# The blocks of w1 by halves of F, and another order of splits, ranks and the tile table around the first tiles

## The chip, the cores and the metric

One NeuronCore of a Trainium2 chip runs the whole kernel, which is written by hand for its five engines: TensorE (PE, matmuls; PEld is its load of weights), VectorE (DVE), ScalarE (ACT), GpSimd (POOL) and SyncE (SP, which here issues DMAs). The metric is the device time in microseconds, the median of several runs.

## The reference

Pooled attention, a routed layer with one expert for each token, and a routed layer with two, in float32:

```python
x = attention(q, pooled k, pooled v)       # 8 x 576 tokens, 512 wide
e = argmax(x @ w_gate + bias); g = softmax(...)[e]
x = g * (relu(x @ w1[e]) @ w2[e])          # layer 1, 8 experts, F = 1024
n = x @ w_gate2 + log1p(exp(x @ w_noise)) * noise
for e in top 2 of n: out += p[e] * (relu(x @ w1b[e]) @ w2b[e])   # layer 2
```

## The kernel before

**Tiles.** Attention runs over 36 tiles of 128 tokens (`t`). Each ends in `av(t)`, whose VectorE part makes `xr` (in two halves) and the gate's logits `lg`, and in `store_x(t)`, a DMA of 256 KB into `x_d`, issued from ScalarE's queue one step later. The gate works by five groups of tiles: `gate_a` makes the one-hot matrix `goh` (VectorE), `gate_b1` the exp (ScalarE) and the ranks (small matmuls, L864 and L866), `gate_b2` and `gate_c` scatter each token's entry into the list `l1_d`. From the list and a table of tiles, the tokens of one expert are gathered 128 at a time: `us[k]`, called tile k here, 37 tiles in layer 1 and 76 in layer 2.

**One tile.** `gather_tile` (GpSimd: copy `cur` out of the list, gather `x`, and in layer 1 gather `nz` and take five small steps), `xT` (transposes of x on TensorE), `g1(u, hf)` for the two halves of F, `hT` or `hT_pe` (transposes of h), `g2` (in the program of the next tile), `finish` (ScalarE: `yo` and the first part of x3; GpSimd: `xr`; SP: a store of yo). The gate of layer 2 needs the result in three bf16 parts: `rest_b` (ScalarE), `rest_c` (GpSimd, L358), `x2T` (SP: the DMA transpose `x3t`), `logits2` (TensorE, L371). Every product of float32 matrices is made of three matmuls of parts (`mm3`, L294 to L296), so every block of weights is split into a high part (ScalarE) and a low part (VectorE for the first expert, GpSimd later): `split_pair` for the first expert's blocks, two at a time, `split_w` for one block of a later one.

**The first expert's weights** are loaded by pairs of blocks (`load_pair`, 512 KB on SP) into three staging buffers `sg`; w1 has pairs 0 to 3, and so has w2. A fourth pair waits for a buffer. w1's high and low parts stand where the buffers of attention's loads were, w2's where attention's other buffers were, the four `xr` among them.

**What sets the order.** The program's order is that of every engine's queue; waits between engines are semaphores, and a waiting instruction holds up all behind it on its engine. The attention loop (from L987) calls the splits of w1 at t = 33, 34 and 35:

```python
for i in {34: (1, 2), 35: (3,)}.get(t, ()):
    split_w1(i)
...
if t == 33:
    split_w1(0)
```

Tiles 0 to 3 are in `opening(k)`: g1 of tile k, with other steps at fixed places, then g2 and finish of tile k-1, hT_pe of tile k, and the three parts of tile k-1. `pre(k)` gathers tile k by the table (a generator; its first step is the gather of x), `prew(k)` loads a weight block. The table of tiles is a generator of small VectorE steps, `tab1`, up to "pe", where TensorE transposes it (L613) and VectorE copies it into `row`; registers of POOL, ACT and SP are loaded from `row` (L174). In `opening(2)` the rest of tab1, pre(4), prew(3) and prew(4) come ahead of g2 of tile 1.

Of the kernel before, what the change touches and what calls it, by code (L numbers as in the profile page):

```python
# [41 lines left out]
def kernel(ctx: ExitStack, tc: tile.TileContext, a: dict):  # L42
# [182 lines left out]
    def load_pair(u, src, j, k):  # L225
        u.sg = stg.tile([P, 2, 512], F32, name="sg")
        nc.sync.dma_start(u.sg, wpair[ds(src + j, 2), :, k, :].rearrange("j p f -> p j f"))
# [70 lines left out]
    def g1(u, hf):  # L298
        if hf == 0:
            u.h = mk.tile([P, F], F32, name="h", bufs=1)  # L300
        p = bank(hf)
        for c in range(4):
            s = slice(c * P, (c + 1) * P)
            mm3(p, u.xh[:, s], u.xl[:, s], 0, u.par + (2 * c + hf), c == 0, c == 3, u.reads)
        A.activation(u.h[:, 512 * hf:512 * hf + 512], p, AF.Relu)  # L305
# [149 lines left out]

    def load_list(src):
        nc.sync.dma_start(lst.rearrange("p c k -> p (c k)"), src.rearrange("(p c) k -> p (c k)", p=P))
# [8 lines left out]
    def first_expert():  # L466
        c = const.tile([P, E], F32, name="fc")
        V.tensor_tensor(c, base1, ebase8, op=OP.subtract)
        m = const.tile([P, 8], F32, name="fm")
        V.max(m, c)  # L470
        ix = const.tile([P, 8], mybir.dt.uint32, name="fix")
        V.max_index(ix, m, c)
        e0 = const.tile([P, 1], F32, name="fe")
        V.tensor_copy(e0, ix[:, 0:1])
        ei = const.tile([1, 2], I32, name="fei")
        V.tensor_scalar(ei[:, 0:1], e0[0:1, :], float(CPE), None, op0=OP.mult)
        V.tensor_scalar(ei[:, 1:2], e0[0:1, :], 8.0, None, op0=OP.mult)
        V.tensor_scalar(p8, iota8, e0, None, op0=OP.subtract)
        V.tensor_scalar(c, p8, 0.0, 8.0, op0=OP.is_lt, op1=OP.mult)
        V.tensor_tensor(p8, p8, c, op=OP.add)  # L480
        V.tensor_scalar(first8, p8, 0.0, None, op0=OP.is_equal)
        return reg(ei[0:1, 0:1], [ET.SP], 7 * CPE), reg(ei[0:1, 0:1], [ET.Pool], 7 * CPE), reg(ei[0:1, 1:2], [ET.SP], 56)

    def tables(layer, base, res, tag=""):
# [128 lines left out]
        nc.tensor.transpose(tp[0:12, 0:P], tab, ident)  # L613
        sc = w.tile([1, 4 + K2], I32, name="sc" + L)
# [17 lines left out]
        yield  # L632
        row = w.tile([6, P], I32, name="row" + L)
        V.tensor_copy(row, tp[0:6, 0:P])
# [49 lines left out]
    with actx:  # L684
# [172 lines left out]

        def gate_b1(g):
            n = GS[g]
            lg, oh = gs[g]  # L860
            A.activation(lg, lg, AF.Exp)
# [74 lines left out]
        def pick_first():  # L936
            at["col"], at["col_p"], at["w"] = first_expert()
# [9 lines left out]
        def load_w1(i):  # L947
# [3 lines left out]
            load_pair(pairs[0][i], at["w"], 2 * i, 0)  # L951
# [39 lines left out]
        for t in range(NT):  # L991
# [4 lines left out]
            for i in {34: (1, 2), 35: (3,)}.get(t, ()):  # L996
                split_w1(i)
# [6 lines left out]
            if t == 33:  # L1004
# [83 lines left out]
    def opening(k):  # L1088
# [9 lines left out]
        if k != 2:  # L1098
            xT(us[k + 1])
        if k == 0:  # L1100
            gate_b1(NG - 1)
        if k == 3:
            split_w(u, 0, u.dst, u.eng)
# [3 lines left out]
        if k == 3:  # L1107
            drain(gate)
        if k == 0:
            gate_b2(NG - 1)  # L1110
# [3 lines left out]
            for i in range(3):  # L1114
                split_pair(pairs[1][i], 2 * i, 1, V)
            load_list(l1_d)
# [4 lines left out]
        if k == 1:  # L1121
            split_pair(pairs[1][3], 6, 1, V)
            drain(until(tab1, "pe"))
        if k == 2:
            drain(tab1)
            drain(pre(4))
            prew(3)
            prew(4)
# [9 lines left out]
        finish(v)  # L1138
        if k == 3:
# [7 lines left out]
        if k == 1:  # L1147
            us[K1].dense = K1
            late = gather_tile(us[K1], lst, at["col_p"] + K1, 1)
# [8 lines left out]
        drain(late)  # L1158

# [140 lines left out]
def host_arrays(inp):  # L1300
# [41 lines left out]
    for g, (w1, w2) in enumerate((("moe_w1", "moe_w2"), ("moe2_w1", "moe2_w2"))):  # L1342
# [3 lines left out]
        w[8 * g:8 * g + 8, :, :, 0] = u.reshape(8, 4, P, 2, 512).transpose(0, 1, 3, 2, 4).reshape(8, 8, P, 512)  # L1346
# [18 lines left out]
```

## Time and profile before

| | |
|---|---|
| median of 3 timed runs | 1483.0 us (1481.58 to 1483.82) |
| the profiled execution | 1486.63 us, its span 1484.9 us |
| mean granted TensorE clock | 0.996 |
| PE, PEld busy | 98%, 81% |
| DVE, ACT, POOL busy | 80%, 81%, 61% |

Times in the profile's rows are microseconds from the span's start. In a timeline the columns are start, duration, engine, line, operation, output <- input, shapes and number of instructions, and in brackets the idle time of the engine ahead of it with what ended it. "issue" is a wait that the profile shows no cause of. A matmul of 128x512 starts some 0.23 us behind the one before; its own duration is longer, since they overlap.

### The profile page before, as it was taken

Reading aid. Unit: us, or ns where it says so; the run is one execution under the profiler, and the core shown is the slowest. Engines: PE = TensorE matmul, PEld = TensorE weight load, DVE = VectorE, ACT = ScalarE, POOL = GpSimd, SP = SyncE. Lnnn points to the kernel's source line nnn. Section 1 sums busy time; section 2 is a strip of 40 time slices with the busy share of each in tenths; the row PEclk is TensorE's granted clock in tenths of the full one; section 3 lists DMA queues with packets and bytes.
Section 4 is the critical chain, followed back from the end, with each engine's and each line's share of the span. In section 5 each row is a group of like instructions: output and inputs, shape, how many; then the busy total and the mean of one; then the engine's idle time right before and its main releaser. Section 6 shows DMA issues by size and latency. Waiting matters only on the chain.

```text
span 1484.9 us, 31025 instructions
## 1 busy us (share of the span) xinstructions
PE 1449.0 (98%) x7485; PEld 1209.0 (81%) x7485; DVE 1181.0 (80%) x2995; ACT 1200.2 (81%) x3153; POOL 900.5 (61%) x1064
## 2 busy tenths in 40 slices
PE   7998899999999999999999999999999999999997
PEld 6988788888888888778888888888888888888886
DVE  6776767777777777779888888888888888888884
ACT  5766559888888888878888888888888888888883
POOL 7677568888888887665544544445445445444452
PEclk9999999999999999999999999999999999999999
DMA  8965555655555554444344344443443443434432
GB/s 320 339 222 181 187 137 146 161 161 147 142 140 140 142 142 135 132 101 107 89 107 93 88 106 93 100 98 89 107 93 86 107 93 92 102 92 104 94 88 45
DMA packets 136891, 191.10 MB, mean 129 GB/s; under 512 B 71376, under 2 KB 95184, under 8 KB 134032
## 3 DMA queue, kind: packets, MB, share of 16 engines
q1 hardware_dynamic: 102240, 129.67, 29.2%
q0 software_dynamic: 24688, 49.94, 17.2%
q10 hardware_dynamic: 9792, 9.44, 1.9%
q8 instruction: 80, 1.31, 0.4%
q14 instruction: 91, 0.75, 0.2%
HBM read 121.64 MB, written 52.82 MB: 117 GB/s over the span
## 4 chain that ended last, share of the span: by engine, by line
issue 36%; PE 33%; POOL 15%; DVE 4%; POOLq 4%; ACT 4%; DMA 2%; SPq 0%; another core or an unknown queue 0%; ACTq 0%; DVEq 0%
PE bank L294 8%; PE bank L296 8%; PE bank L295 8%; POOL out L453 8%; POOL w2l L223 5%; PE bank L817 3%; POOLq L174 3%; PE bank L332 2%; ACT xt L289 2%; PE bank L771 2%; PE bank L798 1%; DMA x_d<-xr 1%; POOLq L223 1%; DVE g2t L393 1%; POOL cur L244 1%
## 5 line engine op out<-in xcount | busy, mean ns | idle before, releaser
L312 DVE STREAM_TRANSPOSE ht<-h 32x256 f32<-32x256 f32 x1136 | 495.4, 436 | 95.9 <-ACT h L305 81.3
L289 ACT ACTIVATE xt<-xz 32x128 f32<-32x128 f32 x1728 | 531.4, 308 | 34.6 <-DVE xz L282 13.5
L294 PE MATMUL bank<-w1h,xh 128*128 (+1 forms) x904 | 357.3, 395 | 0.0
L295 PE MATMUL bank<-w1l,xh 128*128 (+1 forms) x904 | 354.6, 392 | 0.0
L296 PE MATMUL bank<-w1h,xl 128*128 (+1 forms) x904 | 353.7, 391 | 0.0
L296 PE MATMUL bank<-w2h,hl 128*128 (+1 forms) x896 | 351.7, 393 | 0.1
L295 PE MATMUL bank<-w2l,hh 128*128 (+1 forms) x896 | 351.4, 392 | 0.0
L294 PE MATMUL bank<-w2h,hh 128*128 (+1 forms) x896 | 350.6, 391 | 0.0
L223 POOL TENSOR_TENSOR w1l<-sg,w1h 128x512 f32 x109 | 140.7, 1291 | 237.5 <-ACT w1h L220 231.3
L453 POOL DMA_INDIRECT out<-yo,cur x76 | 121.1, 1593 | 163.4 <-ACT yo L450 155.9
L296 PEld LDWEIGHTS bank<-w2h,hl 128*128 128x128 f32 x896 | 168.3, 188 | 39.7 <-DVE hl L321 3.3
L296 PEld LDWEIGHTS bank<-w1h,xl 128*128 128x128 f32 x904 | 169.8, 188 | 36.8
L294 PEld LDWEIGHTS bank<-w1h,xh 128*128 128x128 f32 x904 | 169.7, 188 | 36.3
L295 PEld LDWEIGHTS bank<-w1l,xh 128*128 128x128 f32 x904 | 169.9, 188 | 35.2
L294 PEld LDWEIGHTS bank<-w2h,hh 128*128 128x128 f32 x896 | 168.3, 188 | 37.2
L295 PEld LDWEIGHTS bank<-w2l,hh 128*128 128x128 f32 x896 | 168.3, 188 | 36.4
L305 ACT ACTIVATE h<-bank 128x512 f32<-128x512 f32 x226 | 133.0, 589 | 68.5 <-PE bank L296 59.8
L223 POOL TENSOR_TENSOR w2l<-sg,w2h 128x512 f32 x109 | 141.5, 1298 | 14.3 <-ACT w2h L220 14.3
L250 POOL DMA_INDIRECT x<-x_d,cur x113 | 124.1, 1098 | 37.7 <-POOL cur L244 33.4
L320 ACT ACTIVATE hh<-ht 128x1024 fp32r<-128x1024 f32 x71 | 75.4, 1062 | 58.6 <-DVE ht L312 30.6
L278 DVE TENSOR_TENSOR xl<-xt,xh 128x512 fp32r<-128x512 f32 x108 | 77.2, 715 | 56.0 <-ACT xh L274 43.4
L187 POOL DMA_INDIRECT l_d<-le,dst x74 | 80.1, 1083 | 28.8 <-issue 12.3
(269 smaller groups left out, 1979.2 us busy)
## 6 DMA issues: line engine op xcount, KB each, us to landing
sg<-w SPq DMA_DIRECT2D x118, 512.0 KB
out<-zt SPq DMA_DIRECT2D x37, 256.0 KB
x_d<-yo SPq DMA_DIRECT2D x37, 256.0 KB
x_d<-xr ACTq DMA_DIRECT2D x36, 256.0 KB
kk<-kT SPq DMA_DIRECT2D x7, 1152.0 KB
q<-qT SPq DMA_DIRECT2D x7, 1152.0 KB
vv<-vT SPq DMA_DIRECT2D x7, 1152.0 KB
x_d<-zt SPq DMA_DIRECT2D x10, 256.0 KB
```

What stands on the lines that cost most here:

```text
L187: ins = G.indirect_dma_start(out=dram_t, out_offset=bass.IndirectOffsetOnAxis(ap=ix, axis=0), in_=src, in_offset=None, bounds_check=P * LC ...
L223: eng.tensor_tensor(l, u.sg[:, k, :], h.bitcast(F32), op=OP.subtract)
L250: G.indirect_dma_start(out=u.x, out_offset=None, in_=src[0:top, :], in_offset=off, bounds_check=top - 1, oob_is_err=True)
L278: V.tensor_tensor(u.xl, p, u.xh.bitcast(F32), op=OP.subtract)
L289: A.activation(u.xt[32 * q:32 * q + 32, :, 32 * i:32 * i + 32], zv[:, q], AF.Copy)
L294: nc.tensor.matmul(p, hs, rh, start=first, stop=False)
L295: nc.tensor.matmul(p, hs, rl, start=False, stop=False)
L296: nc.tensor.matmul(p, ls, rh, start=False, stop=last)
L305: A.activation(u.h[:, 512 * hf:512 * hf + 512], p, AF.Relu)
L312: V.transpose(out=t[32 * q:32 * q + 32, :, 32 * i:32 * i + 32], in_=hv[:, q])
L320: A.activation(u.hh, u.t, AF.Copy)
L453: G.indirect_dma_start(out=out_d, out_offset=bass.IndirectOffsetOnAxis(ap=u.ci[:, 2:3], axis=0), in_=u.yo, in_offset=None, bounds_check=N ...
```

## The change

It reorders the host's array of w1 so that blocks 0 to 3 hold half 0 of F and blocks 4 to 7 half 1 (`u.par + 4 * hf + c`); pair 3 of w1 is loaded into the buffer named ht instead of a staging buffer. Pair 0 is split behind av(34), pairs 1 to 3 ahead of av(35). In `opening(0)` the exp of the last gate group and the first two splits of w2 stand ahead of g1's second half, the ranks behind it, and the last two splits behind hT_pe. A new DMA, `load_column`, brings the list's column for tile 3's gather. In `opening(1)` the table's last steps are at the end; in `opening(2)` the rest of the table, pre(4), prew(3) and prew(4) are behind finish of tile 1; in `opening(3)` xT of tile 4 and the first split of tile 3's block are behind g1's second half. `row` is copied ahead of the table's last scalars. Left out below are that copy's place and a register of POOL that is no longer loaded:

```diff
@@ -222,8 +222,11 @@
             h = block(W[2 * k], dst, 0.5)
         eng.tensor_tensor(l, u.sg[:, k, :], h.bitcast(F32), op=OP.subtract)
 
-    def load_pair(u, src, j, k):
-        u.sg = stg.tile([P, 2, 512], F32, name="sg")
+    def load_pair(u, src, j, k, own=False):
+        if own:
+            u.sg = mk.tile([P, 8, P], F32, name="ht", bufs=1).rearrange("p (j k) f -> p j (k f)", j=2)
+        else:
+            u.sg = stg.tile([P, 2, 512], F32, name="sg")
         nc.sync.dma_start(u.sg, wpair[ds(src + j, 2), :, k, :].rearrange("j p f -> p j f"))
 
     def split_pair(u, j, k, eng):
...
@@ -301,7 +304,7 @@
         p = bank(hf)
         for c in range(4):
             s = slice(c * P, (c + 1) * P)
-            mm3(p, u.xh[:, s], u.xl[:, s], 0, u.par + (2 * c + hf), c == 0, c == 3, u.reads)
+            mm3(p, u.xh[:, s], u.xl[:, s], 0, u.par + (4 * hf + c), c == 0, c == 3, u.reads)
         A.activation(u.h[:, 512 * hf:512 * hf + 512], p, AF.Relu)
 
     def hT(u):
...
@@ -452,6 +455,11 @@
     def add_out(u):
         G.indirect_dma_start(out=out_d, out_offset=bass.IndirectOffsetOnAxis(ap=u.ci[:, 2:3], axis=0),
                              in_=u.yo, in_offset=None, bounds_check=N + P - 1, oob_is_err=True, compute_op=OP.add)
+
+    def load_column():
+        col4 = const.tile([P, 8], F32, name="fm")[:, 0:4].rearrange("p (c k) -> p c k", c=1)
+        nc.sync.dma_start(col4, l1_d.rearrange("(p c) k -> p c k", p=P)[:, ds(at["col"] + K1, 1), :])
+        return col4
 
     def load_list(src):
         nc.sync.dma_start(lst.rearrange("p c k -> p (c k)"), src.rearrange("(p c) k -> p (c k)", p=P))
...
@@ -855,10 +862,15 @@
             gate_b1(g)
             gate_b2(g)
 
+        def gate_e(g):
+            lg, oh = gs[g]
+            A.activation(lg, lg, AF.Exp)
+
         def gate_b1(g):
             n = GS[g]
             lg, oh = gs[g]
-            A.activation(lg, lg, AF.Exp)
+            if g < NG - 1:
+                gate_e(g)
             pr = bank(7)[:, 0:(n + 1) * E].rearrange("p (t e) -> p t e", e=E)
             for t in range(n):
                 nc.tensor.matmul(pr[:, t + 1:, :], ones, oh[:, t:t + 1, :].to_broadcast([P, n - t, E]),
...
@@ -948,7 +960,7 @@
             if i == 0:
                 rctx.close()
                 open_w(0, "right")
-            load_pair(pairs[0][i], at["w"], 2 * i, 0)
+            load_pair(pairs[0][i], at["w"], 2 * i, 0, i == 3)
 
         def split_w1(i):
             split_pair(pairs[0][i], 2 * i, 0, V)
...
@@ -993,15 +1005,15 @@
                 transp(t)
             if t == NT - 1:
                 xT(early[0])
-            for i in {34: (1, 2), 35: (3,)}.get(t, ()):
-                split_w1(i)
+                for i in (1, 2, 3):
+                    split_w1(i)
             scores(t + 3, 0)
             maxes(t + 3, 0)
             expo(t + 2)
             if t:
                 store_x(t - 1)
                 av(t)
-            if t == 33:
+            if t == NT - 2:
                 split_w1(0)
             scores(t + 3, 1)
             maxes(t + 3, 1)
...
@@ -1095,37 +1107,37 @@
                 next(gate)
             drain(pr)
         g1(u, 0)
-        if k != 2:
+        if k < 2:
             xT(us[k + 1])
         if k == 0:
-            gate_b1(NG - 1)
+            gate_e(NG - 1)
+            for i in (0, 1):
+                split_pair(pairs[1][i], 2 * i, 1, V)
         if k == 3:
-            split_w(u, 0, u.dst, u.eng)
             drain(until(gate, "tail"))
             xblocks(us[5])
         g1(u, 1)
         if k == 3:
+            xT(us[4])
+            split_w(u, 0, u.dst, u.eng)
             drain(gate)
         if k == 0:
+            gate_b1(NG - 1)
             gate_b2(NG - 1)
             for n in range(GS[-1]):
                 gate_c(NG - 1, n)
             hT_pe(u)
-            for i in range(3):
+            at["col4"] = load_column()
+            load_list(l1_d)
+            for i in (2, 3):
                 split_pair(pairs[1][i], 2 * i, 1, V)
-            load_list(l1_d)
             for n in range(12):
                 next(tab1)
             return
         late = iter(())
         if k == 1:
-            split_pair(pairs[1][3], 6, 1, V)
-            drain(until(tab1, "pe"))
-        if k == 2:
-            drain(tab1)
-            drain(pre(4))
-            prew(3)
-            prew(4)
+            for n in range(6):
+                next(tab1)
         if k == 3:
             drain(xshift(us[5]))
             xhigh(us[5], flat(us[5].xt))
...
@@ -1136,6 +1148,11 @@
             xT(us[3])
         g2(v, range(4, 8))
         finish(v)
+        if k == 2:
+            drain(tab1)
+            drain(pre(4))
+            prew(3)
+            prew(4)
         if k == 3:
             xblocks(us[6])
             hT_pe(u)
...
@@ -1146,7 +1163,7 @@
         hT_pe(u)
         if k == 1:
             us[K1].dense = K1
-            late = gather_tile(us[K1], lst, at["col_p"] + K1, 1)
+            late = gather_tile(us[K1], at["col4"], 0, 1)
         elif k == 2:
             late = pre(5)
         next(late, None)
...
@@ -1156,6 +1173,8 @@
             logits2(us[0])
         x2T(v)
         drain(late)
+        if k == 1:
+            drain(until(tab1, "pe"))
 
     def gated(k):
         u, v = us[k], us[k - 1] if k else None
...
@@ -1343,7 +1362,7 @@
         u = inp[w1]
         if g == 0:
             u = u.reshape(8, 2, 4, D, F).transpose(0, 1, 3, 2, 4)
-        w[8 * g:8 * g + 8, :, :, 0] = u.reshape(8, 4, P, 2, 512).transpose(0, 1, 3, 2, 4).reshape(8, 8, P, 512)
+        w[8 * g:8 * g + 8, :, :, 0] = u.reshape(8, 4, P, 2, 512).transpose(0, 3, 1, 2, 4).reshape(8, 8, P, 512)
         w[8 * g:8 * g + 8, :, :, 1] = inp[w2].reshape(8, 8, P, 512)
     r["w"] = w
     return {k: np.ascontiguousarray(v) for k, v in r.items()}
```

ScalarE's queue around half 1 of tile 0. `w1h` and `w2h` are the high parts in splits of pairs, `x_d<-xr` the stores of x, `lg<-lg` the exp of the gate, `h<-bank` relu of one half, `hh<-bank` the high part of h's transposes. Before:

```order
L231 ACTIVATE w1h<-sg 128x1024
L828 DMA x_d<-xr 256x1x256 x2
L305 ACTIVATE h<-bank_2534 128x512
L274 ACTIVATE xh<-bank_2548 128x512
L861 ACTIVATE lg<-lg 128x40
L305 ACTIVATE h<-bank_2565 128x512
L334 ACTIVATE hh<-bank_2616 128x512
L334 ACTIVATE hh<-bank_2623 128x512
L231 ACTIVATE w2h<-sg 128x1024 x3
```

and now:

```order
L234 ACTIVATE w1h<-ht 128x1024
L835 DMA x_d<-xr 256x1x256 x2
L308 ACTIVATE h<-bank_2531 128x512
L277 ACTIVATE xh<-bank_2545 128x512
L867 ACTIVATE lg<-lg 128x40
L234 ACTIVATE w2h<-sg 128x1024 x2
L308 ACTIVATE h<-bank_2559 128x512
L337 ACTIVATE hh<-bank_2617 128x512
L337 ACTIVATE hh<-bank_2624 128x512
```

Two splits of w2 moved ahead of the second half's h, between it and the exp.

GpSimd's queue around `xr` of tile 1 (with `x_2943` before, with `x_2882` now). The rows from a gather `x<-x_d,cur` to the last `sm<-sm` are one tile's gather with its small steps, and `TENSOR_LOAD` are loads of registers from the table's row. Before, from the gather of tile 4 on:

```order
L250 DMA x<-x_d,cur 128x512
L254 DMA nz<-noise,cur 128x8
L258 COPY le_2882<-cur 128x2x2
L259 ISA
L259 COPY le_2882<-idx_sb 128x2
L261 CAST sm<-cur 128x1
L262 TENSOR_SCALAR sm<-sm 128x1
L263 TENSOR_SCALAR sm<-sm 128x1
L174 TENSOR_LOAD row_2863 x2
L352 TENSOR_TENSOR xr<-yo,x_2943 128x512
L174 TENSOR_LOAD row_2863 x2
L244 ISA
```

and now, from xr of tile 1 on:

```order
L355 TENSOR_TENSOR xr<-yo,x_2882 128x512
L174 TENSOR_LOAD row_2889 x2
L247 ISA
L247 COPY cur<-lst 128x4
L253 DMA x<-x_d,cur 128x512
L257 DMA nz<-noise,cur 128x8
L261 COPY le_2922<-cur 128x2x2
L262 ISA
L262 COPY le_2922<-idx_sb 128x2
L264 CAST sm<-cur 128x1
L265 TENSOR_SCALAR sm<-sm 128x1
L266 TENSOR_SCALAR sm<-sm 128x1
```

The gather of tile 4 moved from ahead of xr of tile 1 to behind it.

The same queue just behind, up to the last part of tile 1's result (`x<-xr,x`), on which its x3t waits. Before:

```order
L352 TENSOR_TENSOR xr<-yo,x_2943 128x512
L174 TENSOR_LOAD row_2863 x2
L244 ISA
L244 COPY cur<-lst 128x4
L250 DMA x<-x_d,cur 128x512
L358 TENSOR_TENSOR x_2943<-xr,x_2943 128x512
```

and now:

```order
L174 TENSOR_LOAD row_2889 x4
L247 ISA
L247 COPY cur<-lst 128x4
L253 DMA x<-x_d,cur 128x512
L361 TENSOR_TENSOR x_2882<-xr,x_2882 128x512
```

The register loads that stood on both sides of xr now stand together, ahead of `cur` of tile 5.

## Rows read from the trace of the kernel before

**Rows 1.** Busy time by stretches: PE, PEld, DVE, ACT, POOL, then PEclk, DMA share, GB/s.

```profile
160.00:180.00 20.00, 14.23 (x93) 12.22 (x94) 14.58 (x51) 10.58 (x24) 11.27 (x18) 1.00 0.58 186
180.00:600.00 420.00, 419.72 (x2366) 349.32 (x2364) 321.31 (x1036) 360.00 (x938) 340.20 (x471) 1.00 0.54 143
```

**Rows 2.** Timeline of TensorE, 163 to 180 us.

```profile
163.59 1.77 PE L817 MATMUL bank<-vb,et 97*128 97x146 f32 x12 [0.94 <-ACT et L799]
...
175.78 0.27 PE L864 MATMUL bank<-goh,tri_bf 128*128 128x40 bf16 x5 [2.82 <-DVE goh L850]
...
179.62 0.66 PE L332 MATMUL bank<-ident_sb,h 128*128 128x128 f32 x4 [0.25 <-ACT h L305]
```

**Rows 3.** Timeline of ScalarE, 162 to 184 us.

```profile
162.06 1.09 ACT L231 ACTIVATE w1h<-sg 128x1024 fp32r<-128x1024 f32 x1
...
178.97 0.60 ACT L305 ACTIVATE h<-bank 128x512 f32<-128x512 f32 x1 [2.86 <-PE bank L296]
...
180.81 2.95 ACT L231 ACTIVATE w2h<-sg 128x1024 fp32r<-128x1024 f32 x3
```

**Rows 4.** Timeline of VectorE, 163 to 176 us.

```profile
163.59 3.67 DVE L232 TENSOR_TENSOR w1l<-sg,w1h 128x1024 fp32r<-128x1024 f32 x3
...
170.28 1.23 DVE L232 TENSOR_TENSOR w1l<-sg,w1h 128x1024 fp32r<-128x1024 f32 x1 [1.01 <-issue]
...
173.36 0.18 DVE L820 RECIPROCAL rs<-bank 128x4 f32<-128x4 f32 x1 [1.27 <-PE bank L268]
...
173.57 0.46 DVE L821 TENSOR_TENSOR xr<-bank,rs 128x288 f32<-128x288 f32 x1
...
175.65 0.20 DVE L851 TENSOR_TENSOR lg<-lg,gm 128x40 f32<-128x40 f32 x1
```

**Rows 5.** Timeline, a store issued on SP and the gather on GpSimd that waited for it.

```profile
642.66 0.34 SPq L348 DMA_DIRECT2D x_d<-yo  x1
...
647.09 1.08 POOL L250 DMA_INDIRECT x<-x_d,cur  x1 [0.88 <-DMA x_d<-yo]
```

**Rows 6.** Timeline of TensorE, 204 to 231 us.

```profile
204.16 1.04 PE L332 MATMUL bank<-ident_sb,h 128*128 128x128 f32 x8
...
208.18 0.60 PE L268 MATMUL bank<-ident_sb,x 128*128 128x128 f32 x4
...
211.38 0.39 PE L294 MATMUL bank<-w2h,hh 128*128 128x512 f32 x1
...
217.75 0.46 PE L371 MATMUL bank<-wg_sb,x3t 128*128 128x48 bf16 x12
...
230.07 0.46 PE L371 MATMUL bank<-wg_sb,x3t 128*128 128x48 bf16 x12
```

**Rows 7.** Timeline of GpSimd, 201 to 214 us.

```profile
201.16 0.19 POOL L244 COPY cur<-lst 128x4 f32 x1 [1.91 <-DVE row L634]
...
201.99 1.10 POOL L250 DMA_INDIRECT x<-x_d,cur  x1 [0.64 <-PE bank L268]
...
205.26 0.19 POOL L263 TENSOR_SCALAR sm<-sm 128x1 f32<-128x1 f32 x1
...
206.00 1.17 POOL L352 TENSOR_TENSOR xr<-yo,x 128x512 f32<-128x512 f32 x1 [0.55 <-ACT x L347]
...
207.90 1.10 POOL L250 DMA_INDIRECT x<-x_d,cur  x1 [0.59 <-POOL cur L244]
...
213.61 0.19 POOL L244 COPY cur<-lst 128x4 f32 x1 [1.14 <-issue]
```

**Rows 8.** Timeline, DMA transposes issued on SP, and the matmuls that waited for the last.

```profile
210.26 1.46 SPq L362 DMA_TRANSPOSE x3t<-x  x1
...
224.98 1.29 SPq L362 DMA_TRANSPOSE x3t<-x  x1
...
596.33 1.45 SPq L362 DMA_TRANSPOSE x3t<-x  x1
...
600.09 0.47 PE L371 MATMUL bank<-wg_sb,x3t 128*128 128x48 bf16 x12 [0.37 <-DMA x3t<-x]
```

More of the change, by code (lines that the diff above doesn't have):

```diff
@@ L481, in first_expert @@
         V.tensor_scalar(first8, p8, 0.0, None, op0=OP.is_equal)
-        return reg(ei[0:1, 0:1], [ET.SP], 7 * CPE), reg(ei[0:1, 0:1], [ET.Pool], 7 * CPE), reg(ei[0:1, 1:2], [ET.SP], 56)
+        return reg(ei[0:1, 0:1], [ET.SP], 7 * CPE), reg(ei[0:1, 1:2], [ET.SP], 56)
     def tables(layer, base, res, tag=""):
@@ L613, in tables @@
         nc.tensor.transpose(tp[0:12, 0:P], tab, ident)
+        row = w.tile([6, P], I32, name="row" + L)
+        V.tensor_copy(row, tp[0:6, 0:P])
         sc = w.tile([1, 4 + K2], I32, name="sc" + L)
@@ L631, in tables @@
             V.tensor_scalar(sc[:, 2:3], tot[0:1, :], 1.0, None, op0=OP.add)
-        yield
-        row = w.tile([6, P], I32, name="row" + L)
-        V.tensor_copy(row, tp[0:6, 0:P])
         res.update(row=row, sc=sc)
@@ L936, in pick_first @@
         def pick_first():
-            at["col"], at["col_p"], at["w"] = first_expert()
+            at["col"], at["w"] = first_expert()
         def snapshot1():
```

## The prediction

> **What bounds the kernel now.** Read the busy time by stretches first. From 180 to 600 us TensorE is busy 419.72 of 420.00 us, while the 20 us ahead of it, where attention ends and the first tiles begin, hold only 14.23 us of matmuls, so 5.77 us of idle [rows 1]. After 180 us TensorE sets the pace, and a stall or a saving made before that shifts all that follows and reaches the end. So two things are to be read: what ends each wait of TensorE between 160 and 180 us, and who has only little slack behind it once it is full.
>
> For the first question the timelines of TensorE, ScalarE and VectorE stand side by side. TensorE waits 0.94 us for `et` [rows 2], because ScalarE splits the first pair of w1 (1.09 us at 162.06) ahead of the two `et` copies [rows 3]. VectorE then makes three low parts of w1 (3.67 us) before the attention output of t=34, sits idle 1.01 us ahead of the fourth low part, and 1.27 us ahead of the second half of t=35 [rows 4]. So the one-hot matrix of the last gate group is late, and TensorE, which has the ranks ahead of half 1 of tile 0, waits 2.82 us [rows 2]. From there to the transposes of `h`, whose second half starts at 179.62, it has only 0.25 us more [rows 2].
>
> For the second question the queue of GpSimd is read, and who uses what it releases. Call E the start of the transposes of tile 2's h, just behind g2 of tile 1: 204.16 [rows 6]. GpSimd makes xr of tile 1 at E+1.84 (206.00), and the DMA transpose x3t of tile 1, which waits for GpSimd's last residue, goes out at 210.26, E+6.10 [rows 7, 8]. TensorE wants it at 217.75, E+13.59 [rows 6]. The next x3t is issued at 224.98 and wanted at 230.07 [rows 6, 8], 5.09 us. How long such a transpose takes shows where TensorE waits for one: issued at 596.33, matmuls at 600.09, 3.76 us [rows 8]. So tile 1 has 7.49 - 3.76 = 3.73 us to spare, tile 2 only 1.33. This is the thin cover behind a full TensorE.
>
> **The change, part by part.** *Pairs by halves, and pair 3 in the ht buffer.* Count and size of matmuls and loads stay; half 0 now needs pairs 0 and 1 alone. Pair 3 no longer waits for a staging slot. No cost: the ht buffer has no user until the tiles that transpose h on VectorE.
>
> *Splits around t=34 and 35, and the ranks.* ScalarE's first split goes behind `et`, and on VectorE t=34 goes ahead of all low parts; four low parts then stand ahead of t=35. VectorE has the same work between 163.59 and the end of its last `xr` (173.57 + 0.46 = 174.03), in another order. Of these 10.44 us, 2.28 were idle: 1.01 for the late fourth pair, 1.27 for a matmul's signal [rows 4]. If neither comes back the last xr ends at 174.03 - 2.28 = 171.75; if both do, at 174.03. Half 1 of tile 0 no longer stands behind the ranks, so TensorE ends it before VectorE ends the gate, and the next to wait for is `h`.
>
> *Two splits of w2 and the exp ahead of h.* Here the change adds a wait. The high parts of w2 are written into space that attention's xr buffers held, and the first of them waits for the landing of the last store of x, which follows that last xr; relu h of half 1 is queued behind two splits on ScalarE, and the transposes of h wait for it. The trace of before has no row for this wait. The nearest is a store of the same 256 KB that somebody waited for: issued at 642.66, its reader starts at 647.09, 4.43 us [rows 5]. From below, the store cannot matter less than not at all: then exp, which follows the gate's last step, is what the splits wait for. That step ended at 175.65 + 0.20 = 175.85, 1.82 us behind the last xr [rows 4], and the exp takes about 0.25. I take 4.4 us, since the row is a store of equal size. So: 171.75 + 4.43 = 176.18; two splits of 2.95/3 = 0.98 each [rows 3], 178.15; h to the transposes 179.62 - 178.97 = 0.65 us [rows 2, 3], 178.80. Against 179.62 this gains **0.8 us**. Ends: with no wait for the store 171.75 + 1.82 + 0.25 + 1.97 + 0.65 = 176.44, a gain of 3.2; with both idles back and the store at 4.4, 181.08, a loss of 1.5.
>
> The Trainium skill prices a DMA at some 2 us fixed plus its bytes over 436 GB/s (DMA: Bandwidth & Descriptors, "Anatomy of one DMA"). By that, as an estimate, this 256 KB store would land in 2.6 us, and the gain would be 2.6 us instead of 0.8; the row of this kernel shows 4.43, and the sum goes by the row.
>
> *Splits 2 and 3 of w2, the column load, the table steps, the row copy.* Nothing: between h of tile 0 and its g2 TensorE has both halves of tile 1 as cover, which hid three splits before and now hide two. If that cover went, g2 of tile 0 would wait for the last low part, some 1.2 us like one of w1's (3.67/3 [rows 4]). The gather of tile 3 reads its column instead of the whole list; TensorE did not wait for it.
>
> *The gather of tile 4 behind finish of tile 1.* Before, GpSimd did this while it had nothing else: `cur` at 201.16, the gather at 201.99, the last small step ending at 205.45, so 4.29 us of engine time ahead of xr of tile 1 [rows 7]. Now xr comes first, and the block, its table row available only behind g2 of tile 1, stands between xr and the gather of tile 5. The four register loads that stood around xr, hidden, now stand together behind the block. Two such loads are what lies in the 1.14 us of "issue" ahead of cur at 213.61 [rows 7]; I charge 1.14 once and take two loads as covered, up to 1.9 if none is. So everything from `cur` of tile 5 on comes 4.29 + 1.14 = 5.4 us later (to 6.2) relative to E. Queued behind it: the residue of tile 1, its x3t on SP, the gather of tile 5, then xr and x3t of tile 2.
>
> Who waits: x3t of tile 1 has 3.73 us to spare, so the logits of tile 1 stall TensorE 5.4 - 3.73 = 1.7 us. xT of tile 4, moved behind half 1 of tile 3, wants its gather at E+6.9 (half 1 of tile 3 ended at 211.38, now about 0.35 earlier, since the transposes no longer stand ahead of it); the gather goes out at E+3.74 (as that of tile 5 did behind xr, 207.90) and, used in time at 208.18 when issued at 201.99, takes at most 6.2 us [rows 6, 7]; at worst a stall of 3.1, which is then part of the stall at the logits and not beside it. Then tile 2: GpSimd has hardly a gap between xr of tile 1 and 225 us, so I give back only about 0.5 of the 5.4; x3t of tile 2 has 1.33 us to spare, so the total shift becomes 4.9 - 1.33 = **3.6 us**. Ends: 1.7 if GpSimd catches up before tile 2, 6.2 - 1.33 = 4.9 if nothing is given back. Later tiles keep the shift but add nothing, since by then both engines are shifted together.
>
> **Sum.** -0.8 + 3.6 = +2.8 us; bounds -3.2 + 1.7 = -1.5 and +1.5 + 4.9 = +6.4. The profiled execution took 1486.63 us for a span of 1484.9, above the median of the three timed runs, 1483.0 (1481.58 to 1483.82); some of its waits, the 1.27 us for a signal first, may not be in those. I add the sum to the median: **1485.8 us**.
>
> **Rivals.** *The opening gains in full.* If half 1's h comes as soon as its matmuls do, with no store in the way, the opening could give most of its 5.77 us: start of the second half near 174.9, 4.8 us earlier. With the smallest loss behind it, -4.8 + 1.7 = -3.1: 1479.9 us. For it: half 0 needs fewer splits and the ranks leave the path. Against: the splits stand ahead of h in ScalarE's own order. 0.12.
>
> *The two halves cancel.* The store lands sooner than the row of 4.43 us, so that the opening gains midway between 0.8 and 3.2, 2.0 us, and GpSimd regains its lag before tile 2: -2.0 + 1.7 = -0.3, 1482.7 us. For it: that row also holds whatever else its reader did after the landing, and GpSimd is idle over a third of the span; against: not in these 20 us. 0.25. The Trainium skill's price of a DMA, named above, would make this rival's gain 2.6 us and its time 1482.1.
>
> *Slower, by GpSimd's queue.* Its register loads are not hidden, its lag is 6.2 us, x3t of tile 2 stalls TensorE to 4.9 us in all, and VectorE's idle for a signal returns, 178.80 + 1.27 = 180.07, a loss of 0.45: +4.9 + 0.45 = +5.35, 1488.4 us. It decides where the lag, less 1.33, exceeds the opening's gain by more than 3 us. For it: two loads alone already cost 1.14 us that nothing hid [rows 7]. Against: two others stood behind a running xr and cost nothing. 0.25.
>
> *The moved work is hidden after all* and nothing changes but the order: -0.8 + 0 = -0.8, 1482.2 us. It would need x3t to have more slack than 3.73 us; no row gives that, and I count it with the second rival.
>
> **Numbers.** The forecast case (+1.5 to +4.2, 1484.5 to 1487.2 us) has 0.38. A measurement here tells 0.2%, 3 us, from no change: 1480.0 to 1486.0 is the same. Half of the forecast case lies above it, with the third rival 0.44 slower; 0.44 same (the other half and the second rival); 0.12 faster. The range 1481.0 to 1488.5 leaves out the first rival and the tail above the third.
>
> **What would show it.** Right: TensorE idle ahead of the second half of h's transposes, released by ScalarE's h, with w2h ahead of it waiting for a DMA; no wait for the one-hot matrix ahead of half 1; logits of tiles 1 and 2 (and xT of tile 4) waiting for x3t and for the gather, 2 to 5 us in all between E and E+30; GpSimd's xr of tile 1 followed by the gather of tile 4. Wrong: no TensorE wait behind g2 of tile 1 (the second term falls), or second-half transposes starting before 177 (the first term was mis-sized), or new stalls after 260 us.

## The result, and the profile after

The changed kernel takes 1490.84 us, the median of 5 runs (1488.37 to 1491.31), against 1481.58 us of before in the same runs (1480.63 to 1483.82). The ratio is 1.0055, 95% interval 1.0043 to 1.0066: **slower by about 8 us** by the ratio (the two medians lie 9.3 us apart). The forecast was 1485.8 us with a range up to 1488.5. The profiled execution took 1490.28 us, its span 1488.5 us.

TensorE's timeline of the changed kernel shows the stages. The first row is the last of attention's score matmuls; then the two halves of tile 0's transposes of h, tile 2's, xT of tile 4, and the logits of tiles 1, 2 and 3.

```profile
156.40 0.65 PE L778 MATMUL bank<-kb,q 128*128 128x144 f32 x4
...
172.63 0.64 PE L335 MATMUL bank<-ident_sb,h 128*128 128x128 f32 x4
178.10 1.12 PE L335 MATMUL bank<-ident_sb,h 128*128 128x128 f32 x4 [4.83 <-ACT h L308]
...
205.11 1.04 PE L335 MATMUL bank<-ident_sb,h 128*128 128x128 f32 x8
...
213.06 0.66 PE L271 MATMUL bank<-ident_sb,x 128*128 128x128 f32 x4 [1.01 <-DMA x<-x_d,cur]
...
220.72 0.47 PE L374 MATMUL bank<-wg_sb,x3t 128*128 128x48 bf16 x12 [0.63 <-DMA x3t<-x]
...
235.34 0.47 PE L374 MATMUL bank<-wg_sb,x3t 128*128 128x48 bf16 x12 [1.62 <-DVE le L417]
...
247.66 0.46 PE L374 MATMUL bank<-wg_sb,x3t 128*128 128x48 bf16 x12
```

The second half of tile 0's transposes waits 4.83 us for h, where it waited 0.25 [rows 2]. Behind g2 of tile 1, TensorE waits for the gather of tile 4, for x3t of tile 1 and ahead of the logits of tile 2, where in before's first profile it waited for none of them [rows 6]. ScalarE's timeline of the changed kernel tells what held h: the issue of the last store, the exp, the two splits of w2, h.

```profile
170.80 0.52 ACTq L835 DMA_DIRECT2D x_d<-xr  x1
...
172.58 0.24 ACT L867 ACTIVATE lg<-lg 128x40 f32<-128x40 f32 x1
175.56 2.00 ACT L234 ACTIVATE w2h<-sg 128x1024 fp32r<-128x1024 f32 x2 [2.74 <-DMA x_d<-xr]
177.47 0.58 ACT L308 ACTIVATE h<-bank 128x512 f32<-128x512 f32 x1
```

The split starts 4.76 us behind the store's issue, released by that store, and h comes 1.9 us later. The second thing to see is the clock. Busy time of the changed kernel by stretches (PE, PEld, DVE, ACT, POOL, then PEclk, DMA share, GB/s):

```profile
175.00:180.00 5.00, 1.90 (x7) 1.71 (x8) 3.22 (x9) 3.73 (x6) 0.00 (x0) 0.70 0.10 24
180.00:185.00 5.00, 5.00 (x18) 3.97 (x17) 4.80 (x17) 2.59 (x4) 2.97 (x3) 0.62 0.22 82
185.00:190.00 5.00, 5.00 (x24) 4.10 (x23) 3.95 (x27) 0.95 (x2) 2.08 (x3) 1.00 0.03 2
```

Behind the idle the granted clock is 0.70 and 0.62, a mixture of its two levels, 1.2 and 2.4 GHz; before it was 1.00 throughout 160 to 180 [rows 1]. Matmuls of half 0 of tile 1 started 0.43 us apart instead of 0.23 (timeline of TensorE):

```profile
179.44 0.63 PE L298 MATMUL bank<-w1l,xh 128*128 128x512 f32 x1
179.87 0.63 PE L299 MATMUL bank<-w1h,xl 128*128 128x512 f32 x1
180.29 0.63 PE L297 MATMUL bank<-w1h,xh 128*128 128x512 f32 x1
```

One stage has to be read from more than one execution, since attention's end comes at 155.5 to 161.7 us in the twelve profiles of this study, with no change there that explains it. So the stages are measured from the start of the last scores (S), to the transposes of tile 2's h (E), to the logits of tile 3 (G). Times in us; the ratio is that to before in the same runs.

| kernel | S to E | E to G | sum | median of runs | ratio, 95% interval |
|---|---|---|---|---|---|
| before, first profile | 45.76 | 38.21 | 83.97 | 1481.6 | |
| before, again | 44.19 | 38.87 | 83.06 | | |
| the change | 48.71 | 42.55 | 91.26 | 1490.8 | 1.0055 (1.0043 to 1.0066) |
| e1 table and gather back | 49.28 | 38.22 | 87.50 | 1486.4 | 1.0023 (1.0011 to 1.0035) |
| e2 splits behind h | 42.01 | 42.69 | 84.70 | 1486.8 | 1.0030 (1.0018 to 1.0043) |
| e3 both | 46.38 | 38.21 | 84.59 | 1484.5 | 1.0013 (1.0002 to 1.0025) |
| e4 fill | 46.12 | 44.22 | 90.34 | 1490.3 | 1.0050 (1.0033 to 1.0067) |
| e5 store elsewhere | 45.12 | 42.56 | 87.68 | 1487.1 | 1.0043 (1.0023 to 1.0063) |
| e6 fill, table back | 46.77 | 38.33 | 85.10 | 1484.6 | 1.0017 (1.0007 to 1.0027) |
| v1 table in mid g2 | 45.25 | 40.33 | 85.58 | 1487.8 | 1.0027 (1.0014 to 1.0041) |
| v2 splits behind g1 | 47.20 | 40.30 | 87.50 | 1486.0 | 1.0026 (1.0013 to 1.0038) |
| v3 fourth split late | 42.61 | 38.22 | 80.83 | 1480.9 | 0.9990 (0.9976 to 1.0005) |

The change is 91.26 - 83.06 = 8.2 us longer than the second profile of before over these two stages, 4.5 us ahead of E and 3.7 behind it, and 7.3 us longer than the first; 0.0055 of 1481.6 us is 8.1. So the loss can be accounted for in these stages. That isn't proof to the microsecond. From G to the end of the span the profiles took from 1238.0 us (v3) to 1243.6 us (v1), two kernels that differ only ahead of G. And before's median was 1481.6 to 1483.4 us in the runs beside which the kernels were timed, so kernels are better compared by the ratio than by their medians.

### The profile page after: what moved, and what is told of

Read it like the earlier page. It is cut to its first block, busy times and chain, and to the rows that moved or that the text cites. A ratio compares the mean times of both kernels' runs of the same rounds, so it can differ in the third digit from the quotient of the medians.

```text
span 1488.5 us, 31026 instructions
## 1 busy us (share of the span) xinstructions
PE 1451.3 (98%) x7485; PEld 1209.1 (81%) x7485; DVE 1179.9 (79%) x2995; ACT 1200.9 (81%) x3153; POOL 901.2 (61%) x1064
## 3 DMA queue, kind: packets, MB, share of 16 engines
q8 instruction: 80, 1.31, 0.4%
## 4 chain that ended last, share of the span: by engine, by line
issue 36%; PE 27%; POOL 15%; DVE 7%; ACT 7%; POOLq 4%; DMA 3%; another core or an unknown queue 0%; SPq 0%; ACTq 0%; DVEq 0%
POOL out L456 8%; PE bank L297 6%; PE bank L299 6%; PE bank L298 6%; POOL w2l L223 5%; ACT xt L292 4%; PE bank L824 3%; POOLq L174 3%; PE bank L778 2%; DMA x_d<-xr 1%; PE bank L335 1%; DVE g2t L396 1%; PE bank L805 1%; POOLq L223 1%; ACT hh L337 1%
```

## The experiments

**A second profile of before.** Expected:

> The kernel before, unchanged, for a second profile of it. It tells what of its first profile recurs. Theory (the signal of TensorE's matmuls that came 1.3 us late at the second half of t=35 is a matter of the execution, not of the order): from the last scores of attention to the second half of tile 0's transposes 19 to 21.2 us (21.22 in the first profile), from there to the transposes of tile 2's h 24.5, from there to the logits of tile 3 38.2. Rival: the same 21.2 again.

Measured, TensorE's timeline of it: the last scores, the ranks, the second half of tile 0's transposes, tile 2's transposes, the logits of tile 3.

```profile
156.75 0.65 PE L771 MATMUL bank<-kb,q 128*128 128x144 f32 x4
...
172.53 0.27 PE L864 MATMUL bank<-goh,tri_bf 128*128 128x40 bf16 x5 [1.24 <-DVE geq L846]
...
176.38 0.66 PE L332 MATMUL bank<-ident_sb,h 128*128 128x128 f32 x4 [0.25 <-ACT h L305]
...
200.94 1.03 PE L332 MATMUL bank<-ident_sb,h 128*128 128x128 f32 x8
...
239.81 0.46 PE L371 MATMUL bank<-wg_sb,x3t 128*128 128x48 bf16 x12
```

From S to the second half it took 19.63 us instead of 21.22, and the wait for the ranks was 1.24 instead of 2.82 [rows 2]. So those 1.6 us are a matter of the execution and not of the kernel's order; how often they come isn't shown. The gain at the opening was worked out from the profile that had them. This execution took 1484.78 us, the first 1486.63. The second profile has a wait of its own, too: x3t of tile 2 goes out at E+22.50 instead of E+20.82 [rows 8], and TensorE waits 0.29 us ahead of the logits of tile 2, 4.06 us behind it (SP, then TensorE):

```profile
223.44 1.29 SPq L362 DMA_TRANSPOSE x3t<-x  x1
...
227.50 0.47 PE L371 MATMUL bank<-wg_sb,x3t 128*128 128x48 bf16 x12 [0.29 <-issue]
```

**e1: the gather of tile 4 and the table back.**

```diff
         if k == 1:
-            for n in range(6):
-                next(tab1)
+            drain(until(tab1, "pe"))
+        if k == 2:
+            drain(tab1)
+            drain(pre(4))
+            prew(3)
+            prew(4)
...
         finish(v)
-        if k == 2:
-            drain(tab1)
-            drain(pre(4))
-            prew(3)
-            prew(4)
...
         drain(late)
-        if k == 1:
-            drain(until(tab1, "pe"))
```

> The changed kernel with the table's steps and the gather of tile 4, prew(3) and prew(4) back ahead of g2 of tiles 0 and 1, as before; nothing else undone. Theory (GpSimd's queue behind g2 of tile 1 costs TensorE 4.3 us by the logits of tile 2: 30.2 us from the transposes of h to those logits where 25.9 stood before): that distance goes back to about 26 us, the waits for x<-x_d (1.0), x3t (0.6) and le (1.6) are gone, and the time falls by 4 us, from 1490.8 to about 1486.5. The idle ahead of the second half of tile 0's transposes stays at 4 to 5 us. Rival (the opening carries the whole loss, the later stalls only take up slack that TensorE had anyway): the time falls by less than 1 us.

1486.38 us, 4.5 below the change, and E to G is 38.22, as before. Shown: the second stage's loss is this part of the change. What it did in the changed kernel is read on GpSimd and SP, its timelines there (xr of tile 1, the gathers of tiles 4 and 5, the residue of tile 1, and the issues of x3t of tiles 1 and 2):

```profile
206.55 1.17 POOL L355 TENSOR_TENSOR xr<-yo,x 128x512 f32<-128x512 f32 x1 [6.20 <-DVE sc L633]
...
208.70 1.11 POOL L253 DMA_INDIRECT x<-x_d,cur  x1 [0.64 <-POOL cur L247]
...
214.32 1.10 POOL L253 DMA_INDIRECT x<-x_d,cur  x1 [0.64 <-PE bank L271]
215.46 1.18 POOL L361 TENSOR_TENSOR x<-xr,x 128x512 bf16<-128x512 f32 x1
...
216.66 1.47 SPq L365 DMA_TRANSPOSE x3t<-x  x1
...
231.30 1.46 SPq L365 DMA_TRANSPOSE x3t<-x  x1
```

E is 205.11, so xr comes at E+1.44, the gather of tile 4 at E+3.59, x3t of tile 1 at E+11.55 and that of tile 2 at E+26.19, where before they were E+6.10 and E+20.82 [rows 8]. The lag of 5.4 us that the prediction charged is 5.45 and 5.37 here. The edit moves the table's steps and two weight loads as well; that it is GpSimd's queue that counts is read from these rows, not from the run alone.

**e2: the first splits of w2 behind the transposes of h.**

```diff
             gate_e(NG - 1)
-            for i in (0, 1):
-                split_pair(pairs[1][i], 2 * i, 1, V)
...
             load_list(l1_d)
-            for i in (2, 3):
+            for i in range(4):
                 split_pair(pairs[1][i], 2 * i, 1, V)
```

> The changed kernel with the first two splits of w2 back behind the transposes of tile 0's h. Theory (relu h of half 1 waits behind these splits for the landing of the last store of x, 4.8 us, and TensorE's idle then costs it the clock at 178 to 184 us): h follows its matmuls at once, the second half starts near 173.5 instead of 178.1, the granted clock stays 1.00 from 175 to 190, together 6 to 7 us less, 1484 to 1485. Rival A (the wait is real, the clock has another cause): only 4.7 us less, 1486, and the 0.70 and 0.81 of the clock stay. Rival B (g2 of tile 0 then waits for the splits): 2 us less or nothing, with a new wait of TensorE for w2l at g2.

S to E fell by 6.7 us to 42.01, as the theory said, all eight transposes ran at once, and the granted clock was 1.00 from 175 to 190, which rules out rival A. The time fell by only 4.0, to 1486.79 us, where 6 to 7 were expected: in that a miss. Its profile was taken in an execution 1.8 us below its median; the rest of the difference is less than what the profiles differ by behind G. E to G stayed at 42.69, so the two losses are separate. It stayed there although the clock fell to 0.66 in 210 to 215, behind a wait of 2.15 us for the gather of tile 4: the wait ahead of the logits of tile 2 was 0.35 us instead of 1.62, so the slower matmuls used up time that TensorE would have waited.

**e5: the last store out of the way.** The order of no queue changes; only the buffer of the last attention tile's xr does.

```diff
-            xr = wk.tile([P, 2, D + E, 4], F32, name="xr", bufs=4)
+            if t == NT - 1:
+                xr = flat(mk.tile([P, 8, P], F32, name="hl", bufs=1))[:, 0:8 * (D + E)]
+                xr = xr.rearrange("p (a d h) -> p a d h", a=2, h=4)
+            else:
+                xr = wk.tile([P, 2, D + E, 4], F32, name="xr", bufs=4)
```

> The changed kernel with the last attention tile's xr in the buffer named hl, which no weight of w2 is written into, so that the first split of w2 no longer waits for the landing of the last store of x; the order of every queue stays. Theory (it is this landing, 4.8 us behind its issue, that holds h): the split starts right behind the exp, h 2.5 to 2.8 us earlier, TensorE's idle at the transposes of h 2 us instead of 4.8, and with so short an idle the clock stays at 1.00; together 2.7 to 5 us less than the changed kernel, 1486 to 1488. Rival (the split waits for w2's own loads as well): the idle stays above 4 us and the time within 1 us of 1490.8.

ScalarE's timeline of e5, the store, the exp and the two splits, and below it TensorE's second half:

```profile
172.88 0.52 ACTq L839 DMA_DIRECT2D x_d<-hl  x1
...
174.64 0.24 ACT L871 ACTIVATE lg<-lg 128x40 f32<-128x40 f32 x1
174.89 2.00 ACT L234 ACTIVATE w2h<-sg 128x1024 fp32r<-128x1024 f32 x2
...
177.43 0.66 PE L335 MATMUL bank<-ident_sb,h 128*128 128x128 f32 x4 [2.09 <-ACT h L308]
```

The split starts right behind the exp, 2.0 us behind the store's issue, and TensorE's idle falls from 4.83 to 2.09 us. So it was this landing that held h, and not w2's own loads. The clock did not stay at 1.00 as expected: it was 0.88 and 0.78 in 175 to 180 and 180 to 185. S to E fell by 3.6 us. The median of the time fell by 3.8, but its runs lie between 1484.0 and 1495.5 us and the interval of its ratio, 1.0023 to 1.0063, holds that of the change, 1.0055, so the gain is shown in the stage and not in the time.

**e4 and e6: the clock by itself.** 20 matmuls that feed nothing, in the gap; in e4 in the changed kernel, in e6 in e1.

```diff
         for b in range(2):
+            if b == 1 and fill:
+                q = bank(6)
+                for n in range(fill):
+                    nc.tensor.matmul(q, u.xh[:, 0:P], block(W[0], 0, None), start=True, stop=True)
             p = bank(4 + b)
...
-            hT_pe(u)
+            hT_pe(u, fill=20)
```

> The changed kernel with 20 matmuls of 128x512 that feed nothing, written to a free bank, on TensorE between the two halves of the transposes of tile 0's h, 4.6 us in a stretch where it sat idle 4.8. h still comes when it did. Theory (the idle costs the clock behind it): granted clock 1.00 from 175 to 190, half 0 of tile 1 in 2.8 us instead of 5.1, 2.3 us less: 1488.5. Rival (clock and idle are unrelated, or the fill delays the transposes): 1490.8 or up to 1 us more, with the clock still down at 178 to 184.

> The 20 empty matmuls of e4 put into e1, where the table and the gather of tile 4 stand as before and TensorE has no stall behind g2 of tile 1. In e4 the granted clock stayed at 1.00 and the stretch from the second half of tile 0's transposes to those of tile 2's h fell from 27.0 to 24.4 us, yet the time fell by only 0.5 us, and the stretch behind it grew from 42.6 to 44.2. Theory (the clock's 2.5 us are real, and in e4 GpSimd's late queue took most of them back): here they reach the end, that stretch falls from 27.1 to 24.5, the next one stays at 38.2, and the time falls from 1486.4 by 2.5 us to about 1484. Rival (the clock is worth nothing at the end): 1486 again.

Busy time by stretches of e4, columns as above:

```profile
175.00:180.00 5.00, 4.55 (x28) 3.59 (x28) 3.15 (x12) 1.32 (x3) 3.14 (x10) 1.00 0.82 276
180.00:185.00 5.00, 5.00 (x25) 3.88 (x24) 3.22 (x9) 4.21 (x6) 0.00 (x0) 1.00 0.08 29
185.00:190.00 5.00, 5.00 (x25) 4.11 (x24) 4.82 (x17) 2.61 (x5) 2.99 (x3) 1.00 0.21 77
```

The fill keeps the clock at 1.00 in these stretches. From the second half of tile 0's transposes to E it took 24.39 us in e4 and 24.38 in e6, against 27.01 in the change, 27.07 in e1 and 24.54 before: the clock behind the idle costs 2.5 to 2.7 us there. The times show it less plainly. In e6 the median is 1.8 us below e1's (1486.38 to 1484.56), where 2.5 was expected, but the intervals of the two ratios overlap. In e4 it is 0.5 us below the change, where 2.3 was expected, and E to G grew from 42.55 to 44.22.

The expectation of e6 puts that growth down to GpSimd's late queue. The rows say otherwise: behind E, GpSimd was no later in e4 than in the change. x3t of tile 2 went out at E+26.27 in e4 (233.74) and at E+26.19 in the change, and the logits of tile 2 came at E+30.30 and E+30.23. The growth lies behind them. TensorE's logits of tiles 2 and 3 in e4, and two stretches of e4, columns as above:

```profile
237.77 0.47 PE L378 MATMUL bank<-wg_sb,x3t 128*128 128x48 bf16 x12 [1.98 <-DVE le L421]
...
251.69 0.46 PE L378 MATMUL bank<-wg_sb,x3t 128*128 128x48 bf16 x12
...
235.00:240.00 5.00, 3.02 (x28) 2.42 (x27) 3.55 (x13) 4.85 (x15) 4.14 (x8) 0.88 0.78 183
240.00:245.00 5.00, 5.00 (x19) 4.02 (x18) 4.08 (x11) 4.69 (x14) 4.27 (x5) 0.78 0.15 53
```

From one to the other it took 13.92 us, against 12.32 in the change (235.34 to 247.66), where the clock stayed at 1.00 behind its wait of 1.62 us. So the fill kept the clock up behind one idle, and in this execution it fell behind the next, of 1.98 us. Whether it did so in the other runs of e4 isn't shown: the profiled one, 1492.62 us, is 2.3 above their median.

**e3: both parts undone.** Both edits above, e1's and e2's.

> Both edits: splits of w2 behind the transposes of h, table and gather of tile 4 ahead of g2. What is left of the change: blocks by halves, pair 3 in the ht buffer, splits of w1 around t=34 and 35, ranks behind half 1. Theory (two losses that add up, and a gain of the remaining parts at the end of attention): 1490.8 - 4.3 - 6.5 = 1480, some 1 to 3 us below the kernel before (1481.6). Rival (what is left costs as well): 1483 or more.

1484.48 us, and not 1480: a miss. A new wait stands in it. Timelines of e3, TensorE's transposition of the table, VectorE's last split of w2, and ScalarE's:

```profile
194.11 0.28 PE L621 MATMUL bank<-ident_sb,tab_t 128*12 128x128 f32 x1 [2.35 <-DVE tab_t L618]
...
181.69 1.23 DVE L235 TENSOR_TENSOR w2l<-sg,w2h 128x1024 fp32r<-128x1024 f32 x1 [2.60 <-ACT w2h L234]
...
180.60 1.06 ACT L234 ACTIVATE w2h<-sg 128x1024 fp32r<-128x1024 f32 x1 [3.15 <-DMA sg<-w]
```

The fourth pair of w2 is loaded last; ScalarE waits 3.15 us for it, VectorE 2.60 us, and the table's steps, which don't need it, stand behind it on VectorE. TensorE then waits 2.35 us for the table, and the granted clock was 0.91 over 190 to 210. The change had put this split ahead of the table's steps, and the prediction priced that at nothing.

**v1 and v2: the table later, the splits earlier.** v1 is e3 with the table's transposition and the gather of tile 4 in the middle of g2 of tile 1; v2 is v1 with two splits behind half 1's h.

```diff
         if k == 1:
             drain(until(tab1, "pe"))
-        if k == 2:
-            drain(tab1)
-            drain(pre(4))
-            prew(3)
-            prew(4)
...
         g2(v, range(4))
         if k == 2:
             xT(us[3])
+            drain(tab1)
+            drain(pre(4))
+            prew(3)
+            prew(4)
```

> As e3, but the transposition of the table, the gather of tile 4, prew(3) and prew(4) stand in the middle of g2 of tile 1, behind xT of tile 3, instead of ahead of it. In e3 TensorE waited 2.35 us for the table ahead of g2 of tile 1, and the clock was 0.91 over the 20 us behind that wait. Theory (the remaining parts give 4 us at the opening, and e3 lost it again by that wait and the clock behind it): no wait for tab_t, clock 1.00 from 190 to 210, from the second half of tile 0's transposes to those of tile 2's h 25 us instead of 29.1, no waits for x3t or x<-x_d at tiles 1 to 4, and a time of 1480 to 1481, 2 us below before. Rival (GpSimd then runs late as in the changed kernel): waits for x<-x_d and x3t of 1 to 3 us, 1483 or more.

> As v1, but the first two splits of w2 directly behind g1's second half of tile 0 (behind its h on ScalarE, ahead of the transposes' high parts). It tells whether the splits hurt by standing ahead of h, or by holding up ScalarE at all. Theory (only what stands behind the waiting split on ScalarE is late, and the high parts of h have 6 us of cover before g2 of tile 0): TensorE has no wait at the transposes of h, the splits still wait for the store, and the time is that of v1 within 1 us, with VectorE's table steps ending up to 2 us earlier. Rival: g2 of tile 0 waits for hh or hl, 1 to 3 us more than v1.

v1 took 1487.77 us, another miss. The table is no longer waited for, but `hl` of tile 1, which stands behind the table's steps on VectorE (v1, TensorE in g2 of tile 1):

```profile
195.85 0.50 PE L299 MATMUL bank<-w2h,hl 128*128 128x512 f32 x1 [2.59 <-DVE hl L338]
```

and the logits of tile 2 waited 1.38 us, so moving the transposition only moved the wait. v2, at 1485.97, is not told from v1 (the intervals cover one another). It shows that a split that waits doesn't hold up the transposes when it stands behind h: all eight of tile 0 ran at once there, at 174.27. Harmless it isn't shown to be. S to E is 1.95 us longer than in v1, TensorE waited in g2 of tiles 0 and 1, and the clock was 0.82 and 0.84 in 195 to 200 and 200 to 205 (v2, TensorE):

```profile
183.01 0.51 PE L299 MATMUL bank<-w2h,hl 128*128 128x512 f32 x1 [0.96 <-DVE hl L338]
...
197.36 0.50 PE L299 MATMUL bank<-w2h,hl 128*128 128x512 f32 x1 [2.10 <-DVE tab_t L618]
```

**v3: the fourth split where it was.** e3, with

```diff
-            for i in range(4):
+            for i in range(3):
                 split_pair(pairs[1][i], 2 * i, 1, V)
...
         if k == 1:
+            split_pair(pairs[1][3], 6, 1, V)
             drain(until(tab1, "pe"))
```

> As e3, but the fourth split of w2 back behind the table's first 12 steps (in tile 1), as before. In e3 VectorE sat idle 2.6 us for that split, whose pair is loaded last, with all table steps queued behind it, and TensorE then waited 2.35 us for the table. Theory: the table is ready 2 to 2.6 us earlier, that wait of TensorE is gone or below 0.5 us, the clock stays 1.00 from 190 to 210, and the time is 1480 to 1481, 4 us below e3 and 1.5 to 2.5 below before. Rival (VectorE is the limit with all its other work): the wait at the table stays above 1.5 us and the time at 1483 to 1485.

TensorE's transposition of the table and VectorE's last step ahead of it, in v3:

```profile
198.16 0.27 PE L621 MATMUL bank<-ident_sb,tab_t 128*12 128x128 f32 x1
...
197.94 0.14 DVE L618 TENSOR_SCALAR tab_t<-j_t 128x1 f32<-128x1 f32 x1
```

No wait for the table, only one of 0.65 us for that split in g2 of tile 0; S to E is 42.61 and E to G 38.22, the shortest sum of all, 3.8 below e3's. 1480.88 us is 3.6 below e3 (the two intervals overlap at their ends) and 0.9 below before (1481.8 in these runs); the ratio of 0.9990 has an interval that holds 1, so it may be no faster than before.

## Why the prediction was wrong

**The opening's term, -0.8 us, is the step that failed.** From S to E it was 48.71 - 45.76 = +2.9 us against the first profile of before, from which it was worked out, and +4.5 against the second. It was short in the work ahead of the store (1.0 us), a little in the store's landing (0.3) and in the clock (2.5), and against the second profile in its base as well (1.6).

*The base.* It was worked out from an execution of before that held 1.6 us of waits which the second one did not. The prediction said that the 1.27 us for a signal might not be in the timed runs, and then added a gain made partly of them to the median of those runs.

*The work ahead of the store.* It took 1.0 us longer from S to the end of the last xr than the 13.35 us worked out (170.31 + 0.46 = 170.77, less 156.40, is 14.37). The working let both old idles vanish, 2.28 us. VectorE's timeline of the changed kernel shows new idles where old ones went, for t=34's matmuls, for xh and for w1h, 1.12 us together:

```profile
162.01 0.18 DVE L827 RECIPROCAL rs<-bank 128x4 f32<-128x4 f32 x1 [0.55 <-PE bank L824]
...
165.16 0.69 DVE L281 TENSOR_TENSOR xl<-bank,xh 128x512 fp32r<-128x512 f32 x1 [0.31 <-ACT xh L277]
166.11 2.36 DVE L235 TENSOR_TENSOR w1l<-sg,w1h 128x1024 fp32r<-128x1024 f32 x2 [0.26 <-ACT w1h L234]
...
170.31 0.46 DVE L828 TENSOR_TENSOR xr<-bank,rs 128x288 f32<-128x288 f32 x1
```

In the second profile of before the last xr ended 14.02 us behind S (170.77, less 156.75), so against that one the new order brought this step no gain at all.

From the last xr to the second half it took 7.33 us, where 4.43 + 1.97 + 0.65 = 7.05 was worked out. So the landing, priced by the nearest row, was nearly right: 4.76 against 4.43 us. The Trainium skill's 2 us plus bytes over 436 GB/s (DMA: Bandwidth & Descriptors, "Anatomy of one DMA") gives 2.6 for it as an estimate, 2.2 less than this row; the section measured it on DMAs issued by GpSimd, and this store was issued from ScalarE's queue. Another page of the Trainium skill (Perfetto Trace Analysis, "DMA Instruction — HWDGE (DVE, Sync)") says that the signal of a write into HBM can come late, since it follows the write's completion; no row here parts the signal from the transfer.

*The clock.* No term stood for it. The prediction itself had TensorE idle for nearly 4 us, from the end of half 1 to the transposes, and took that stretch at its length alone. It cost 2.5 us more behind it, by the stretches of e4 and e6.

**GpSimd's term, +3.6 us, was right in its mechanism and a little short.** E to G grew by 4.3 against the first profile of before and 3.7 against the second, and e1 took 4.3 away. The lag of 5.4 us held, but the 0.5 us taken as given back before tile 2 was not: 5.37 of it still stood at that tile's x3t. And x3t took 4.04 us from its issue to the logits of tile 2 (231.30 to 235.34) instead of 3.76, so tile 2 had only 5.09 - 4.04 = 1.05 us to spare: 5.37 - 1.05 = 4.3. Against the second profile, whose x3t of tile 2 was itself late and had nothing to spare, the lag is 26.19 - 22.50 = 3.7, and so is the growth. The wait at the logits of tile 1 is smaller than forecast since xT of tile 4 took 1.01 us of it. Ahead of the logits of tile 2 the profile names VectorE's `le`, but the 4.04 us from x3t's issue are those of tile 1 (216.66 to 220.72, 4.06), where it names x3t, and `le` is no input of the logits; so x3t is the likelier, as the prediction had it.

**The third rival**, slower by GpSimd's queue with a loss at the opening, was the nearest by its time, 1488.4, but that is luck: the lag was 5.4 us and not its 6.2, and VectorE's idle of 1.27 us for a signal, from which it had 0.45 us of loss at the opening, did not come back. The rival that the opening gains in full was 1479.9; e2 shows that stage at 42.01 us, 2.2 below before's second profile, and v3 at 42.61, so what the other parts of the change give at the opening is real, and the two splits ahead of h gave it away.

**Splits 2 and 3 of w2 "at nothing"** was right in the changed kernel, where TensorE wanted the table only behind g2 of tile 1, and wrong as soon as that slack went: 3.6 us between e3 and v3.

## What to carry to other kernels

Before work is moved ahead of a waiting engine's input, ask of the first instruction of it what it waits for (a buffer's last reader, a DMA's landing), since all behind it on that queue waits as well, and price TensorE's idle with what the clock can cost behind it. Place work in a queue by when its own input lands: the last pair loaded belongs behind the steps that don't need it. And take a base from more than one profile: a wait that belongs to one execution is no gain to be had.

## What the runs showed of the hardware

TensorE's clock fell behind an idle of 4.83 us (0.70 and 0.62 in the two stretches) and behind one of 2.09 (0.88 and 0.78), while before's first profile kept 1.00 behind 2.82 us [rows 1, 2]. It fell behind 1.98 us in e4 and behind 2.35 in e3 (0.68 in 195 to 200), and stayed at 1.00 behind 2.59 in v1. So the length of the idle alone doesn't tell it here.

A short step of VectorE took several times its length when it met a tensor operation of GpSimd. The same step (L396) in the changed kernel, alone and beside GpSimd's residue, in the timelines of VectorE and GpSimd:

```profile
210.35 0.17 DVE L396 SCALAR_TENSOR_TENSOR g2t<-g2t 128x8 f32<-128x8 f32 x1
...
229.97 1.35 DVE L396 SCALAR_TENSOR_TENSOR g2t<-g2t 128x8 f32<-128x8 f32 x1
...
230.09 1.19 POOL L361 TENSOR_TENSOR x<-xr,x 128x512 bf16<-128x512 f32 x1
```

0.17 us against 1.35, ending together with GpSimd's at 231.3. This is no cost of the change alone: in before too this step takes 1.31 us beside that residue (L393 at 223.67). The Trainium skill (SBUF — State Buffer, "SBUF: two separate sides") says that some VectorE operations and GpSimd's take turns at one pair of ports, each for a whole instruction; the trace agrees with it in that the two end together.
